# Writing the parts of q straight into the stacked operands of a rotary attention and gated MLP kernel

## The chip, the cores and the metric

The kernel runs on one core of a Trainium2 chip. The metric is the device time of one execution in microseconds (us), in which the inputs already lie in the chip's memory.

## What is computed

The reference, cut to what matters:

```python
# q, k, v: [8, 8, 576, 64] (batch, heads, positions, head size), float32
q_rot, k_rot = rotate(q), rotate(k)          # rotary embedding, halves of 32
scores = (q_rot @ k_rot.T) / sqrt(64)
attn = exp(scores - max(scores)); attn /= sum(attn) + 1e-9
x = concat_heads(attn @ v)                   # [8, 576, 512]
h = relu(x @ w_in)                           # [8, 576, 1024]
u, vv = h[..., :512], h[..., 512:]
vn = (vv - mean(vv)) / sqrt(var(vv) + 1e-6)  # over the 512 features
vs = w_spatial @ vn + b_spatial              # mixes the 576 positions
out = (u * vs) @ w_out                       # [8, 576, 512]
```

## The kernel before

The work is cut into 32 pairs of heads, four a batch, and eight MLPs, one a batch. TensorE (PE) makes every product; VectorE (DVE) takes row maxima, transposes the exponentials in blocks of 32 and scales; ScalarE (ACT) makes the exponentials, evacuates PSUM and rounds; GpSimd (POOL) multiplies by the rotary tables and subtracts; SyncE (SP) issues the transfers, from one queue, in order.

**High and low parts.** From pair 4 on, and in the whole MLP, a float32 operand is used as two shorter numbers: a high part, which ACT makes by copying into a rounded type (`round_hi`, line 424), and a low part, which is the operand minus its high part (`rest_lo`, line 427, on POOL). A product is high*high + low*high + high*low.

**Stacks.** A head has 64 rows, PE takes 128. So the two parts of one head's q stand above each other in one operand, and so do two copies of k's high part. For each head a of a pair:

- `qs[a]`: 64 rows of q's high part (the head's own rows) and 64 rows of its low part (the other rows), 512 positions;
- `ks[a]`: k's high part twice; `lks[a]`: k's low part on the own rows, zeros on the others.

`qs[a]` and `ks[a]` are two ranges of one wide tile, `stk0` for head 0 and `stk1` for head 1; both `lks` lie in `stk2`. They exist once, so pair i can fill them only when the scores of pair i - 1 have been made. The last 64 positions of each head don't fit into the four tiles of 128 and go together into one more tile: `qt` (high) and `ql` (low), multiplied with `lk` itself. That tile's scores come first in a pair, then four tiles for head 0 and four for head 1 (line 796).

**Preparing a pair** (`prepare`, from line 525). q and k of a pair are loaded into `st[0]` and `st[1]` (pool `stage`, three buffers for all pairs), each with its half-swapped copy in the columns from 576 on. POOL multiplies both by the tables (two operations of 576 columns, line 549) and adds them (line 553). ACT then rounds, POOL subtracts. For q the high part went to the upper columns of `st[0]` and the low part over the lower ones; for k both go to `lk`. From there ten transfers a pair fill the stacks: four of 128 KB for q, six of 144 KB for k. Four small ACT operations copy the end pieces of q into `qt` and `ql`.

**Order.** Each engine works through its instructions in program order. The order is written out: the table `ORDER` lists all operations by number, a letter behind a number names the engine where there is a choice, and `HOME` lists which buffer of its pool each new tile takes. An operation that has to wait holds up everything behind it on its engine, or on SyncE's queue.

Of the kernel before, what the change touches and what calls it, by code (L numbers as in the profile page):

```python
# [8 lines left out]
F32 = mybir.dt.float32  # L9
# [6 lines left out]
P = 128  # L16
# [79 lines left out]
def pool_ns(n):  # L96
# [4 lines left out]
6 5 2 3 0 9 8 1 12 4 7 11 135 13 137 136 61 63 67 10 68 69 70 139 141 71 72 73 140 74 75 138g 76 33 77 211 78 81 82 79 80 83 84 142g 85 86 87 88 89 90  # L101
15 305 16 17 144 147 212 145 215 42 97 14 98a 18 19 95 56 96a 93 94a 127 128 91 92a 100 101a 62 296 109 110a 99 143 494 306 20 21 104 307 129 102 213
103v 216 146 148 214 105a 106 107a 149 34 57 123 35 152 124a 118 108 150 153 151 36 37 120 38 39 121a 119a 59 309 311 154 24 25 115 116a 157 113 114a
111 26 117 155 158 27 28 29 30 156 112 130 122 125 58 159 126 162 22 167 160 217 218 168a 23 171 172v 163 161 164 165 166 169 173 174v 220 223 408 60
221 170a 287 40 203 204 205 219 176 177a 182 180 131 224 178 179v 222 175 308 185 225 181a 183a 184 43 228 226 186a 199 31 44 45 310 200v 229 418 132
187 51 133 46 47 48 424 227 425 426 430 134 189 390 190a 399 191 192a 230 231 188 49 194 41 195v 196 197a 232 193 198 233 64 206 207 431 417 234 235
238 201 202 503 243 239 236 237 240 245 246a 432 244v 241 247 312 248v 252 50 242 279 253v 256 249 280 254 208 255a 250a 209 288 289 281 314 441 315
316 317 318 210 251 257v 445 261 258 259a 262a 319 52 290 291 292 260 419 427 320 433 321 440 428 293 294 270 429 271a 322 323 267 268v 263 265 297
748 272 298 266a 324 434 436 755 269 264 754 756 273v 299 325 326 327 282 275 435 749 438 274 337 437 328 54 442 276v 341 329 300 301 302 342a 760 303
338v 283 277 278 330 331 757 334 439 332 313 339 340a 333 335 336 373 443 343 344v 444 446 447 448 53 352 353v 350 351a 374 761 375 450 409 410 295  # L110
284 348 451 758 345 452 304 759 349v 411 762 381 355 412 458 413 356a 459 449 346 347a 454 285 286 364 365a 455 354 764 765 453 824 460 359 357 360a
366 461 456 457 358 361 462 463 376 362a 377 830 825 466 467 363 369 367a 368 414 464 465 370a 371 468 469 372 831 470 471 420 421 422 382 423 378 763
# [139 lines left out]
    "11410020117631100051000131604005002120450000010076103100411001350101624000000000511700641100115600571400015200100720004100601750100101001137"  # L252
    "41051100010010170001041062011101001750110401310002150200074000720000401165007011200117132600101400071030000610501104704001100651000150700042"
    "60000116075401012032010051306100110500470000110010110612325400071001001031040026501000146070003001500401130060107011214630000700115440001160"
    "50011400702046360176541322756102153276142501607435164257406517423765406174501"
)


# [865 lines left out]
```

## Time and profile before

| what | value |
|---|---|
| median of three runs | 825.38 us (823.13 to 827.4) |
| the profiled execution: its own time | 820.87 us |
| its span, from first to last instruction | 818.6 us |
| PE / DVE / ACT / POOL busy | 98% / 69% / 65% / 69% of the span |
| granted TensorE clock | 0.997 of full speed |
| data moved by the transfer queue | 142.04 MB |

PE's busy time is that of its matmuls; loading the weights of the next matmul (PEld) overlaps it. Where a row names a releaser, it is what ended the wait, judged from the semaphores; "issue" means that the profile shows nothing that the engine waited for. Times in the rows are from the start of the span.

### The profile page before, as it was taken

Reading aid. Unit: us, or ns where it says so; the run is one execution under the profiler, and the core shown is the slowest. Engines: PE = TensorE matmul, PEld = TensorE weight load, DVE = VectorE, ACT = ScalarE, POOL = GpSimd, SP = SyncE. Lnnn points to the kernel's source line nnn. Section 1 sums busy time; section 2 is a strip of 40 time slices with the busy share of each in tenths; the row PEclk is TensorE's granted clock in tenths of the full one; section 3 lists DMA queues with packets and bytes.
Section 4 is the critical chain, followed back from the end, with each engine's and each line's share of the span. In section 5 each row is a group of like instructions: output and inputs, shape, how many; then the busy total and the mean of one; then the engine's idle time right before and its main releaser. Section 6 shows DMA issues by size and latency. Waiting matters only on the chain.

```text
span 818.6 us, 30242 instructions
## 1 busy us (share of the span) xinstructions
PE 799.3 (98%) x12568; PEld 722.2 (88%) x12568; DVE 561.6 (69%) x1134; ACT 535.6 (65%) x1380; POOL 567.7 (69%) x480
## 2 busy tenths in 40 slices
PE   7999999999999999999999999999999999999998
PEld 3666799998999989999999989999789988999898
DVE  5878997776866676667866579776676657764320
ACT  4998787666866578555865568666576657754442
POOL 6999897965958768665888566878468755823231
PEclk9999999999999999999999999999999999999999
DMA  9665766678767786779768679777856678562101
GB/s 356 231 214 164 182 184 175 164 192 218 193 179 189 195 215 161 175 174 235 189 173 210 160 202 216 174 194 189 226 139 168 176 186 220 126 140 79 44 2 58
DMA packets 62667, 144.56 MB, mean 177 GB/s; under 512 B 10945, under 2 KB 11201, under 8 KB 62530
## 3 DMA queue, kind: packets, MB, share of 16 engines
q1 hardware_dynamic: 62386, 142.04, 65.5%
q8 instruction: 99, 1.62, 0.9%
q10 hardware_dynamic: 144, 0.59, 0.2%
q14 instruction: 38, 0.31, 0.1%
HBM read 93.55 MB, written 9.58 MB: 126 GB/s over the span
## 4 chain that ended last, share of the span: by engine, by line
PE 84%; DMA 6%; SPq 3%; DVE 2%; POOL 2%; ACT 2%; issue 1%; ACTq 0%; POOLq 0%; DVEq 0%
PE psum L796 16%; PE psum L756 14%; PE psum L955 13%; PE psum L970 12%; PE psum L937 11%; PE psum L914 10%; PE psum L816 3%; PE psum L725 3%; SPq L421 3%; PE psum L679 2%; DMA st<-in_qk_dram 1%; DMA rb<-rt20d 1%; DMA stk<-lk 1%; DMA tabs<-in_tab_dram 1%; POOL st L549 1%
## 5 line engine op out<-in xcount | busy, mean ns | idle before, releaser
L838 DVE TENSOR_REDUCE nmx<-psum 128x1 f32<-128x576 f32 x288 | 212.8, 747 | 94.0 <-PE psum L796 78.8
L841 ACT ACTIVATE et<-psum,nmx 128x576 f32<-128x576 f32 x288 | 212.7, 740 | 90.0 <-DVE nmx L838 87.9
L843 DVE STREAM_TRANSPOSE et<-et 128x576 f32<-128x576 f32 x252 | 187.2, 761 | 40.5 <-ACT et L841 40.1
L549 POOL TENSOR_TENSOR st<-st,tabs 128x576 f32<-128x576 f32 x112 | 158.5, 1429 | 52.0 <-DMA st<-in_qk_dram 44.7
L756 PE MATMUL psum<-et,vr 32*64 32x144 f32 x8064 | 141.6, 285 | 0.9 <-issue 0.9
L756 PEld LDWEIGHTS psum<-et,vr 32*64 32x64 f32 x8064 | 126.3, 130 | 12.3 <-issue 10.3
L955 PE MATMUL psum<-wsp,vn 128*128 128x288 f32 x768 | 125.5, 296 | 0.0
L937 PE MATMUL psum<-x,wi 128*128 128x288 f32 x768 | 121.1, 296 | 0.3 <-ACT vn L424 0.2
L970 PE MATMUL psum<-g,wo 128*128 128x288 f32 x768 | 119.2, 296 | 1.1 <-issue 1.1
L914 PE MATMUL psum<-wi,x 128*128 128x512 f32 x448 | 118.0, 396 | 1.8 <-ACT vv L988 1.1
L937 PEld LDWEIGHTS psum<-x,wi 128*128 128x128 f32 x768 | 108.9, 188 | 4.7 <-issue 1.6
L970 PEld LDWEIGHTS psum<-g,wo 128*128 128x128 f32 x768 | 107.8, 188 | 3.8 <-issue 3.0
L955 PEld LDWEIGHTS psum<-wsp,vn 128*128 128x128 f32 x768 | 109.5, 188 | 1.5 <-issue 1.2
L796 PE MATMUL psum<-stk 128*128 128x288 f32 x448 | 99.2, 303 | 4.2 <-ACT et L841 1.5
L796 PE MATMUL psum<-stk,stk 128*128 128x288 f32 x448 | 96.3, 296 | 0.7 <-issue 0.6
L914 PEld LDWEIGHTS psum<-wi,x 128*128 128x128 f32 x448 | 79.5, 188 | 16.8 <-ACT x L772 1.6
L796 PEld LDWEIGHTS psum<-stk 128*128 128x128 f32 x448 | 72.5, 188 | 13.9 <-issue 4.9
L427 POOL TENSOR_TENSOR g<-u,g 128x288 fp32r<-128x288 f32 x64 | 51.1, 806 | 47.7 <-ACT g L424 47.7
L553 POOL TENSOR_TENSOR st<-st 128x576 f32<-128x576 f32 x56 | 79.7, 1427 | 2.9
L880 POOL TENSOR_TENSOR x<-x,rb 128x576 f32<-128x576 f32 x32 | 45.7, 1429 | 40.5 <-DVE nmx L838 10.2
L796 PEld LDWEIGHTS psum<-stk,stk 128*128 128x128 f32 x448 | 71.5, 188 | 0.3 <-DMA stk<-lk 0.3
L427 POOL TENSOR_TENSOR x<-x,x 128x576 fp32r<-128x576 f32 x64 | 54.5, 874 | 18.1 <-ACT x L424 17.9
(129 smaller groups left out, 1020.2 us busy)
## 6 DMA issues: line engine op xcount, KB each, us to landing
vr<-in_v_dram SPq DMA_DIRECT2D x116, 320.0 KB
st<-in_qk_dram SPq DMA_DIRECT2D x64, 576.0 KB
stk<-lk SPq DMA_DIRECT2D x168, 144.0 KB
stk<-st SPq DMA_DIRECT2D x112, 128.0 KB
out_dram<-ob SPq DMA_DIRECT2D x31, 288.0 KB
ws<-in_w_spT_dram SPq DMA_DIRECT2D x2, 576.0 KB
tabs<-in_tab_dram ACTq DMA_DIRECT2D x1, 576.0 KB
wi12raw<-in_w_in_dram SPq DMA_DIRECT2D x1, 512.0 KB
```

What stands on the lines that cost most here:

```text
L427: eng.tensor_tensor(out=lo, in0=src, in1=hi.bitcast(F32), op=ALU.subtract)
L549: f = lambda e: e.tensor_tensor(out=st[j][:, cols], in0=st[j][:, cols], in1=tabs[:, cols], op=ALU.mult)
L553: f = lambda e: e.tensor_tensor(out=st[j][:, :S], in0=st[j][:, :S], in1=st[j][:, S:2 * S], op=ALU.add)
L756: nc.tensor.matmul(bank(g)[64 * h:64 * h + 64, EACH // 9 * (1 - h):EACH // 9 * (1 - h) + EACH], lhsT=vr[rows, b % 4, b // 4, h, :], rhs=e[ ...
L796: nc.tensor.matmul(pt[:, c * 512:c * 512 + HALF], lhsT=lhsT, rhs=rhs[:, c * HALF:(c + 1) * HALF], start=(n == 0), stop=(n == len(parts) - 1))
L838: op(DVE, 680, key + K_MAX, lambda: nc.vector.tensor_reduce(out=nmx.tile, in_=tops(), op=ALU.max, axis=AX.XY, negate=True), r=[pt], w=[nmx ...
L841: op(ACT, 750, key + K_EXP, lambda: nc.scalar.activation(weights(), tops(turn), AF.Exp, bias=nmx.tile, scale=1.0, accum_out=sm[:, to:to + ...
L843: op(DVE, 705, key + K_TURN, lambda: nc.vector.transpose(out=blocks(et, at), in_=blocks(et, at)), w=[(et, at)])
L914: nc.tensor.matmul(pm.tile, lhsT=lhsT, rhs=win[1, d][:, j, :], start=(d == 0 and n == 0), stop=(d == 3 and n == len(todo) - 1))
L937: nc.tensor.matmul(pm[:, :HALF], lhsT=win[0, d][:, i, f * P:(f + 1) * P], rhs=x[d][:, at:at + HALF], start=(d == 0 and n == 0), stop=(d == ...
L955: nc.tensor.matmul(pm[:, :HALF], lhsT=lhsT, rhs=rhs, start=(t == 0 and n == 0), stop=(t == 4 and n == 1))
L970: nc.tensor.matmul(pm[:, :HALF], lhsT=wout[d,][:, i, m * P:(m + 1) * P], rhs=gs[d][:, at:at + HALF], start=(d == 0 and n == 0), stop=(d == ...
```

## The change

For pairs 4 to 31, `prepare` no longer makes q's parts inside `st[0]`. ACT rounds the 512 columns of each head straight into the own rows of `qs[a]`, and POOL writes the difference straight into the other rows, so that the four q transfers of a pair are gone; the six k transfers stay. The end pieces go from `st[0]` into `qt` by ACT and, as differences, into `ql` by POOL (formerly ACT copied both). `st[0]` is free when the last of these eight operations has read it. The operations are numbered and ordered anew (`ORDER`, `HOME`). In the first row of `wake`, `count` is a number for the maker of the order and not part of the program.

```diff
 ORDER = """
-6 5 2 3 0 9 8 1 12 4 7 11 135 13 137 136 61 63 67 10 68 69 70 139 141 71 72 73 140 74 75 138g 76 33 77 211 78 81 82 79 80 83 84 142g 85 86 87 88 89 90
...
+6 5 9 2 3 1 4 8 135 12 7 11 13 136 10 137 139 140 141 138g 142g 309 219 67 68 73 69 70 71 72 74 75 76 77 78 81 82 79 80 83 84 85 86 87 88 144 89 90 0
...
-        def hi(j, rows=slice(0, P)):
-
-            return st[0][rows, S:].bitcast(F32R) if j == 0 else lk[rows, S:]
-
-        def lo_q(e):
-            rest_lo(e, st[0][:, :S].bitcast(F32R), st[0][:, :S], hi(0))
-
-        def tails(part, to, one):
-            for h in range(2):
-                c0 = S * part + 4 * P * (1 - h)
-                one(sixteens(to, h), st[0][64 * h:64 * h + 64, c0:c0 + TW].bitcast(F32).rearrange("p (g i) -> p g i", g=4))
+        own, oth = (lambda a: slice(64 * a, 64 * a + 64)), (lambda a: slice(64 - 64 * a, P - 64 * a))
+        body = lambda a: st[0][own(a), a * TW:a * TW + 4 * P]
+        ends = lambda a: st[0][own(a), 4 * P * (1 - a):4 * P * (1 - a) + TW].rearrange("p (g i) -> p g i", g=4)
+
+        def high_ends():
+            for a in range(2):
+                round_hi(sixteens(qt, a), ends(a))
+
+        def low_ends(e):
+            for a in range(2):
+                rest_lo(e, sixteens(ql, a), ends(a), sixteens(qt, a))
...
-        op(ACT, 573, key - K_HIQ, lambda: round_hi(hi(0), st[0][:, :S]), r=[(st[0], 0)], w=[(st[0], 1)])
-        op(ACT, 535, key - K_TAIL, lambda: tails(1, qt, round_hi), r=[(st[0], 1)], w=["qt"])
-        pair_op(S, key - K_LOQ, lo_q, r=[(st[0], 1)], w=[(st[0], 0)])
-        op(ACT, 535, key - K_TAIL + 0.1, lambda: tails(0, ql, round_hi), r=[(st[0], 0)], w=["ql"])
...
-            for dst, rows, part, tok, dep in (
-                (qd, own, 1, ("qs", a, 0), (st[0], 1)), (kd, own, 1, ("ks", a, 0), (lk, 1)), (kd, oth, 1, ("ks", a, 1), (lk, 1)),
-                (ld, own, 0, ("lks", a), (lk, 0)), (qd, oth, 0, ("qs", a, 1), (st[0], 0)),
-            ):
...
+        op(ACT, 535, key - K_TAIL, high_ends, r=[(st[0], 0)], w=["qt"])
+        op(POOL, 2 * pool_ns(TW), key - K_TAIL + 0.1, lambda: low_ends(nc.gpsimd), r=[(st[0], 0), "qt"], w=["ql"], port=True)
         for a in range(2):
...
+            op(ACT, act_ns(4 * P), key - K_HIQ, lambda a=a: round_hi(qs[a][own(a), :], body(a)), r=[(st[0], 0)], w=[("qs", a, 0)])
+            op(POOL, pool_ns(4 * P), key - K_LOQ, lambda a=a: rest_lo(nc.gpsimd, qs[a][oth(a), :], body(a), qs[a][own(a), :]), r=[(st[0], 0), ("qs", a, 0)], w=[("qs", a, 1)], port=True)
...
+            for dst, rows, part, tok in ((kd, own(a), 1, ("ks", a, 0)), (kd, oth(a), 1, ("ks", a, 1)), (ld, own(a), 0, ("lks", a))):
...
-    op(PE, 3600, -90, wake, r=[("wsp", 0)], w=[idle], new=[idle], count=8)
+    op(PE, 3600, -90, wake, r=[("wsp", 0)], w=[idle], new=[idle], count=16)
```

What the new order does is seen best at two places. The first is SyncE's queue where it fills the stacks for pair 26; `st26_0` is that pair's q, `lk26` its k, and the number behind a name is a buffer's. Before:

```order
L421 DMA stk1_561<-st26_0_8846 64x512
L421 DMA stk2_562<-lk26_9389 64x576 x2
L421 DMA stk1_561<-lk26_9389 64x576
L421 DMA stk0_560<-st26_0_8846 64x512 x2
L421 DMA stk1_561<-lk26_9389 64x576
L421 DMA stk0_560<-lk26_9389 64x576
L421 DMA stk1_561<-st26_0_8846 64x512
L421 DMA st28_0_9721<-in_qk_dram 128x1152
L421 DMA st28_1_9724<-in_qk_dram 128x1152
```

The same place on the same queue in the changed kernel:

```order
L419 DMA vr25_9323<-in_v_dram 32x4x640
L419 DMA stk0_415<-lk26_9397 64x576 x2
L419 DMA stk1_416<-lk26_9397 64x576
L419 DMA stk2_417<-lk26_9397 64x576 x2
L419 DMA stk1_416<-lk26_9397 64x576
L419 DMA st27_0_9621<-in_qk_dram 128x1152
L419 DMA st28_0_9646<-in_qk_dram 128x1152
```

The four copies out of `st26_0` are gone, the two k copies for head 0 come first instead of fourth and last, and the loads behind them have changed places.

The second place is POOL around pairs 22 and 23, beside the MLP of batch 4 (`vn`, the normalised features, are its low parts). Before, with line 427 as the subtraction that makes q's low part inside `st23_0`:

```order
L549 TENSOR_TENSOR st23_0_7759<-st23_0_7759,tabs_64 128x576 x2
L427 TENSOR_TENSOR vn_71<-vv4_2_7824,vn_71 128x512
L553 TENSOR_TENSOR st23_0_7759<-st23_0_7759 128x576
L549 TENSOR_TENSOR st23_1_7893<-st23_1_7893,tabs_64 128x576
L427 TENSOR_TENSOR st23_0_7759<-st23_0_7759 128x576
L549 TENSOR_TENSOR st23_1_7893<-st23_1_7893,tabs_64 128x576
L553 TENSOR_TENSOR st23_1_7893<-st23_1_7893 128x576
L427 TENSOR_TENSOR vn_71<-vv4_3_7848,vn_71 128x512
L427 TENSOR_TENSOR lk23_8098<-st23_1_7893,lk23_8098 128x576
```

The same place on POOL in the changed kernel, with line 425 as the subtractions, line 547 as the products and 551 as the sums:

```order
L425 TENSOR_TENSOR stk1_416<-st22_0_7224,stk1_416 64x512
L547 TENSOR_TENSOR st23_1_7918<-st23_1_7918,tabs_64 128x576
L425 TENSOR_TENSOR stk0_415<-st22_0_7224,stk0_415 64x512
L547 TENSOR_TENSOR st23_1_7918<-st23_1_7918,tabs_64 128x576
L551 TENSOR_TENSOR st23_1_7918<-st23_1_7918 128x576
L425 TENSOR_TENSOR vn_71<-vv4_3_7817,vn_71 128x512
L425 TENSOR_TENSOR lk23_8063<-st23_1_7918,lk23_8063 128x576
```

The low part of pair 22's q now goes into the stacks at the time when the next pair's k is being turned, and for head 0 it stands behind the first product of that k, `st23_1`. Pair 30 is alike, with one more subtraction between:

```order
L547 TENSOR_TENSOR st31_1_11058<-st31_1_11058,tabs_64 128x576
L425 TENSOR_TENSOR vn_71<-vv6_2_11004,vn_71 128x512
L425 TENSOR_TENSOR stk0_415<-st30_0_10440,stk0_415 64x512
L425 TENSOR_TENSOR vt1_72<-vv6_4_11053,vt1_72 64x512
L425 TENSOR_TENSOR x28_11074<-x32_28_10873,x28_11074 128x576
```

There the stacks' row was moved behind the first product of `st31_1`, the k of pair 31.

## Rows read from the trace of the kernel before

**Rows 1.** The page: span, busy times, transfer queues, chain by engine.

```profile
span 818.6 us, 30242 instructions
...
PE 799.3 (98%) x12568; PEld 722.2 (88%) x12568; DVE 561.6 (69%) x1134; ACT 535.6 (65%) x1380; POOL 567.7 (69%) x480
...
q1 hardware_dynamic: 62386, 142.04, 65.5%
...
PE 84%; DMA 6%; SPq 3%; DVE 2%; POOL 2%; ACT 2%; issue 1%; ACTq 0%; POOLq 0%; DVEq 0%
```

**Rows 2.** Windows: start and end in us, length, each engine's busy us.

```profile
12.00:96.00 84.00, 81.22 (x605) 52.59 (x606) 72.34 (x119) 74.88 (x189) 77.56 (x65) 0.98 0.67 218
96.00:800.00 704.00, 696.31 (x11839) 651.90 (x11838) 482.88 (x1004) 452.64 (x1176) 482.71 (x398) 1.00 0.68 172
```

**Rows 3.** PE's waits from 20 us on: total us, times, longest us.

```profile
PE psum L796 <- ACT et L841: 2.0, 3, 1.2
PE psum L796 <- issue: 1.4, 2, 0.8
PE psum L796 <- DMA stk<-lk: 1.3, 1, 1.3
PE psum L914 <- ACT vv L988: 1.1, 1, 1.1
...
PE psum L725 <- DMA vr<-in_v_dram: 0.6, 1, 0.6
PE psum L796 <- DMA rt18d<-rt: 0.4, 1, 0.4
...
PE psum L816 <- issue: 0.2, 1, 0.2
```

**Rows 4.** The stacks' tile view: q transfers, min/median/max ns of an issue.

```profile
L421 SPq DMA_DIRECT2D stk<-st x112: 461/588/1465, 50.1 to 726.5; - x112
```

**Rows 5.** SyncE's timeline from 590 to 606 us: start us, us.

```profile
597.28 0.48 SPq L421 DMA_DIRECT2D stk<-st  x1
...
599.73 1.25 SPq L421 DMA_DIRECT2D stk<-st  x2
```

**Rows 6.** PE's timeline from 600 to 607 us; brackets: idle before, releaser.

```profile
605.48 0.50 PE L796 MATMUL psum<-stk 128*128 128x288 f32 x2 [1.27 <-DMA stk<-lk]
```

**Rows 7.** Groups by shape: busy us, mean ns of one; idle before, releaser.

```profile
L549 POOL TENSOR_TENSOR st<-st,tabs 128x576 f32<-128x576 f32 x112 | 158.5, 1429 | 52.0 <-DMA st<-in_qk_dram 44.7 <-DMA rb<-rt19d 6.9
L427 POOL TENSOR_TENSOR st<-st 128x576 fp32r<-128x576 f32 x28 | 39.9, 1426 | 11.6 <-ACT st L424 11.5
L424 ACT ACTIVATE st<-st 128x576 fp32r<-128x576 f32 x28 | 19.0, 677 | 5.8 <-POOL st L553 5.8
L424 ACT ACTIVATE ql<-st 64x64 fp32r<-64x64 f32 x56 | 14.0, 250 | 2.7 <-POOL st L427 2.3
L427 POOL TENSOR_TENSOR x<-x,x 128x64 fp32r<-128x64 f32 x32 | 10.4, 324 | 0.0
L427 POOL TENSOR_TENSOR vt<-vv,vt 64x512 fp32r<-64x512 f32 x8 | 10.3, 1287 | 11.7 <-ACT vt L424 11.4
L424 ACT ACTIVATE vt<-vv 64x512 fp32r<-64x512 f32 x16 | 9.5, 625 | 0.2
```

**Rows 8.** One window, columns as in rows 2 (POOL is the last engine).

```profile
60.00:180.00 120.00, 117.29 (x1777) 101.65 (x1779) 103.46 (x198) 91.41 (x232) 106.52 (x86) 1.00 0.69 179
```

**Rows 9.** VectorE's transposes: min/median/max ns, first and last start.

```profile
L843 DVE STREAM_TRANSPOSE et<-et x252: 720/768/781, 82.1 to 745.3; 128x576 f32<-128x576 f32 x126
```

**Rows 10.** Waits of all engines: total us, times, longest us.

```profile
POOL st L549 <- DMA st<-in_qk_dram: 44.7, 16, 7.5
...
ACT qt L424 <- PE psum L796: 7.4, 3, 4.2
```

**Rows 11.** Timelines of SyncE and POOL at one load of k.

```profile
473.01 0.35 SPq L421 DMA_DIRECT2D st<-in_qk_dram  x1
477.60 2.83 POOL L549 TENSOR_TENSOR st<-st,tabs 128x576 f32<-128x576 f32 x2 [2.93 <-DMA st<-in_qk_dram]
```

More of the change, by code (lines that the diff above doesn't have):

```diff
@@ L105 @@
[L105 to L108, printed above, removed]
@@ new lines @@
+15 16 17 93 97 94a 147 98a 211 212 95 96a 381 14 18 215 145 56 91 92a 148 19 100 101v 146 109 110a 33 99 59 127 305 102 103a 62 20 213 104 21 390 128
+105v 129 51 24 106 107a 34 216 57 35 149 42 123 152 306 143 124a 153 108 150 151 120 121a 36 37 60 38 217 218 39 25 118 119a 22 154 157 115 116a 113
+114a 26 158 111 155 117 122 27 28 29 311 130 58 156 296 125 30 112 126 159 162 310 160 167 171 172v 168a 164 165 169 170v 214 287 163 161 173 220 221
+223 307 417 166 203 174a 222 224 204 131 132 176 177a 178 179v 133 61 175 63 185 205 418 23 180 182 183a 181v 206 207 43 44 225 228 226 186a 424 134
@@ new lines @@
+229 227 184 399 425 426 40 45 199 200v 187 46 492 47 191 192a 48 65 31 189 190a 230 231 233 188 194 32 196 193 195a 312 197a 232 198 235 238 236 430
+201 234 434 240 241 202 435 239 237 243 245 249 246a 244v 308 250v 247 254 242 208 279 252 255v 280 248a 288 431 209 253a 289 281 41 256 408 314 317
+318 315 316 432 419 210 251 257v 282 428 427 261 429 258 319 259a 260 49 50 290 291 433 746 292 52 262a 265 320 321 293 294 267 53 322 323 436 439 442
+268v 270 271v 263 264 324 438 297 298 272 273a 266v 325 326 269 299 275 276a 274 327 437 747 300 301 328 341 342a 277 313 329 334 278 295 302 303 330
@@ L243 @@
+331 337 332 338v 333 339 340a 335 444 445 336 343 440 350 448 373 344v 352 753 351a 374 375 446 353a 409 410 348 449 752 756 450 447 345 355 304 820
+356a 456 754 755 758 349v 441 346 452 347a 411 359 457 458 364 365a 412 453 454 443 413 283 284 354 361 414 757 464 285 460 360v 286 362a 764 465 366
+376 377 367a 461 466 357 358 826 363 759 382 451 369 370a 766 767 459 420 421 422 368 765 371 768 462 372 455 463 468 469 378 470 379 472 473 474 467
[128 rows of a table added]
 """
 HOME = (
-    "07001001200210320112100321201701101262005314263544564504017201570341170151074205451200106107120672100013167465345740101501260002341620100436"
@@ new lines @@
+    "65230010600541201200105030147100011416010511300001702006001470001100006117300051140011306017140102607000002600700312154010710510615004002010"
+    "61610000524000000311450001000017610200401711061230001007110050040601001241100300221400720006010001175040010010260172010110104610710113600171"
+    "00001104540111560017020507100461100104020176010010001156010112001011140600000700000016130501101140011702003101150700402700010600051001131741"
+    "00160153207031000157440000001102006545110700110001401601062070002130500107163001141007120131400071000020601070002101000154311200076201010170"
@@ new lines @@
+    "14006000371006200001154207600105010001013215700041104000110506115400110700010104062010761000123610540001100011170600401021110701016011050110"
+    "00410701013065110010000016200004501020045000107012610010410012200730154100007001016050110014147500060100014020070002600006171540011202010170"
+    "36000401110710100001106000151002701311060410200010001631500423005000040107011610501016101007140006012100000007104501102570161040001402007662"
+    "00010001500161041720011105030600110000540017011600010000132511207430011011060015400001623005400011070061100031140011572300004100007116045014"
@@ L256 @@
+    "10051700101057406074651202756420317125007621513647065724261574603574601547160"
 )
@@ L564, in prepare @@
                 rope(j, slice(*part), eng)
-        op(ACT, 573, key - K_HIQ, lambda: round_hi(hi(0), st[0][:, :S]), r=[(st[0], 0)], w=[(st[0], 1)])
-        op(ACT, 535, key - K_TAIL, lambda: tails(1, qt, round_hi), r=[(st[0], 1)], w=["qt"])
-        pair_op(S, key - K_LOQ, lo_q, r=[(st[0], 1)], w=[(st[0], 0)])
-        op(ACT, 535, key - K_TAIL + 0.1, lambda: tails(0, ql, round_hi), r=[(st[0], 0)], w=["ql"])
-        op(ACT, 573, key - K_HIQ, lambda: round_hi(hi(1), st[1][:, :S]), r=[(st[1], 0), (st[1], 1)], w=[(lk, 1)], new=[lk])
@@ L571, in prepare @@
-        pair_op(S, key - K_LOK, lambda e: rest_lo(e, lk[:, :S], st[1][:, :S], hi(1)), r=[(st[1], 0), (lk, 1)], w=[(lk, 0)])
-        for a in range(2):
-            own = slice(64 * a, 64 * a + 64)
-            oth = slice(64 - 64 * a, P - 64 * a)
-            qd, kd, ld = lambda a=a: qs[a], lambda a=a: ks[a], lambda a=a: lks[a]
-            for dst, rows, part, tok, dep in (
-                (qd, own, 1, ("qs", a, 0), (st[0], 1)), (kd, own, 1, ("ks", a, 0), (lk, 1)), (kd, oth, 1, ("ks", a, 1), (lk, 1)),
-                (ld, own, 0, ("lks", a), (lk, 0)), (qd, oth, 0, ("qs", a, 1), (st[0], 0)),
-            ):
-                def copy(dst=dst, rows=rows, own=own, part=part, src=dep[0], c0=a * TW if dst is qd else 0, n=4 * P if dst is qd else S):
-                    load(dst()[rows, :].bitcast(F32), src[own, S * part + c0:S * part + c0 + n].bitcast(F32))
-                op(DMA, dma_ns(132, 1, 570, 2.9), key - (K_STACK2 if a else K_STACK), copy, r=[dep], w=[tok])
+        op(ACT, 535, key - K_TAIL, high_ends, r=[(st[0], 0)], w=["qt"])
@@ new lines, in prepare @@
+        op(POOL, 2 * pool_ns(TW), key - K_TAIL + 0.1, lambda: low_ends(nc.gpsimd), r=[(st[0], 0), "qt"], w=["ql"], port=True)
+        for a in range(2):
+            op(ACT, act_ns(4 * P), key - K_HIQ, lambda a=a: round_hi(qs[a][own(a), :], body(a)), r=[(st[0], 0)], w=[("qs", a, 0)])
+            op(POOL, pool_ns(4 * P), key - K_LOQ, lambda a=a: rest_lo(nc.gpsimd, qs[a][oth(a), :], body(a), qs[a][own(a), :]), r=[(st[0], 0), ("qs", a, 0)], w=[("qs", a, 1)], port=True)
+        high = lambda: lk[:, S:]
@@ new lines, in prepare, with copy @@
+        op(ACT, 573, key - K_HIQ, lambda: round_hi(high(), st[1][:, :S]), r=[(st[1], 0), (st[1], 1)], w=[(lk, 1)], new=[lk])
+        pair_op(S, key - K_LOK, lambda e: rest_lo(e, lk[:, :S], st[1][:, :S], high()), r=[(st[1], 0), (lk, 1)], w=[(lk, 0)])
+        for a in range(2):
+            kd, ld = lambda a=a: ks[a], lambda a=a: lks[a]
+            for dst, rows, part, tok in ((kd, own(a), 1, ("ks", a, 0)), (kd, oth(a), 1, ("ks", a, 1)), (ld, own(a), 0, ("lks", a))):
+                def copy(dst=dst, rows=rows, part=part, a=a):
+                    load(dst()[rows, :].bitcast(F32), lk[own(a), S * part:S * part + S].bitcast(F32))
+                op(DMA, dma_ns(132, 1, 570, 2.9), key - (K_STACK2 if a else K_STACK), copy, r=[(lk, part)], w=[tok])
```

19 lines of the change are left out of this document (2 added, 17 removed), and 258 rows, old and new, of the table ORDER.

## The prediction

> **What bounds the kernel now.** I read the page first: the span is 818.6 us, TensorE (PE) is busy in 98% of it, and each of the other engines in 65 to 69% [rows 1]. The chain that ended last is PE work for 84%. Then I cut the span into stretches [rows 2]. From 12 to 96 us PE, ScalarE (ACT) and GpSimd (POOL) are all nearly full: 81.2, 74.9 and 77.6 of 84 us. From 96 to 800 us PE is busy 696.3 of 704 us and everything else has room: POOL 482.7, ACT 452.6, VectorE (DVE) 482.9. So in the long middle PE sets the pace. The change adds and removes no matmul, and all that it could give back is PE's idle time: 84.0 - 81.2 = 2.8 us before 96 us and 704 - 696.3 = 7.7 us after, 10.5 us together. A change beside PE can cost more than that, since nothing bounds how long PE may be made to wait.
>
> Then I asked for whom PE waits [rows 3]: 2.0 us for exponentials on ACT, 1.1 us for ACT's evacuations of the MLP, 1.3 + 0.4 + 0.6 = 2.3 us for transfers, and in five lines, of which the first and the last stand there, 4.3 us that the profile puts down to nothing ("issue"). After the start PE never waits for POOL. Both sides of the change can be read from that: transfers cost PE 2.3 us now, POOL nothing.
>
> **What the change removes.** 112 transfers of 128 KB on SyncE's queue, four for each of the pairs 4 to 31. An issue holds that queue 588 ns in the median [rows 4]: 112 x 0.588 = 65.9 us less in the queue. The data is 112 x 128 KB = 14.7 MB of the queue's 142 MB, about a tenth of what keeps the DMA engines busy in 65.5% of the span [rows 1]. That is worth something only where PE ends up waiting for the queue. The clearest such place is at 605.5 us: PE sat idle 1.27 us for a transfer of k into the stacks [rows 6]. In front of it the queue issued a run of copies without a pause from 597.28 us on, among them q copies at 597.28 and two at 599.73 us [rows 5]. Those three are 0.48 + 1.25 = 1.73 us, more than the 1.27 us that PE waited. The order of the changed kernel has only the six k transfers there, so I take these 1.3 us as gained. The 0.4 us for a row of reciprocals and the 0.6 us for a tile of v go through the same queue, and I count them too: -2.3 us. The bounds are 0 (the next k transfer may wait for its own data) and all three.
>
> ACT loses 28 roundings of 128x576 (19.0 us) and 56 end pieces into ql (14.0 us); POOL loses 28 subtractions of 128x576 (39.9 us) [rows 7].
>
> **What it adds.** ACT rounds twice 64x512 per pair. The nearest row is the 64x512 rounding into vt, 625 ns: 56 x 0.625 = 35.0 us. ACT's sum is 35.0 - 19.0 - 14.0 = +2.0 us, 0.07 us per pair: nothing, with 704 - 452.6 = 251 us idle in the middle [rows 2].
>
> POOL subtracts twice 64x512 per pair. Its row of 64x512 takes 1287 ns, that of 128x576 over twice the partitions 1426 [rows 7]: the columns are paid for and not the partitions, so that splitting one operation by head nearly doubles it. 56 x 1.287 = 72.1 us. The ends are 56 pieces of 64x64; the nearest row is 128x64 with 324 ns, so 18.1 us. POOL's sum is 72.1 + 18.1 - 39.9 = +50.3 us, 1.8 us per pair: the largest term of the change, and it is on an engine that PE does not wait for now. What covers it is POOL's idle time, 704 - 482.7 = 221 us in the middle. The cover is thin in one stretch: from 60 to 180 us POOL is busy 106.5 of 120 us [rows 8], which leaves 13.5 us. The turned pairs' transposes run from 82.1 to 745.3 us [rows 9], so a pair takes some 663 / 28 = 23.7 us, and 120 us bring 5.1 pairs or 9.1 us. It fits if two thirds of the idle time can be used; if half can (6.7 us), POOL ends 2.4 us late there. I take 0 for this stretch, bounds 0 and 2.4.
>
> **What it moves.** The stacks for q exist once. Before, what waited for the previous pair's last scores was a copy on SyncE's queue; now ACT and POOL wait themselves, and whatever stands behind them on these engines waits too. By the order 31 of the 56 new ACT writes carry a wait for PE. Behind them stand exponentials and evacuations, but these feed a PE that is by then at the scores waited for. ACT already stops so three times, 7.4 us in all, at qt [rows 10], and PE loses at most the 2.0 us of [rows 3]. I take 0; the bound is that 7.4 us becomes PE's, were nothing else queued on PE.
>
> Worse is what stands ahead of a new subtraction. In pair 22 the subtraction for head 0 now stands behind the first product of the next pair's k, which needs a fresh load; in pair 30 likewise, with one product and a 128x512 subtraction between. POOL waited for such loads 16 times, 44.7 us in all [rows 10], 2.8 us each; one load was issued at 473.01 us and POOL went on with it at 477.60 us, 4.6 us later [rows 11]. A product takes 1.43 us [rows 7]. If PE stood at the scores when POOL began to wait, each place would cost 2.8 + 1.4 = 4.2 us; if POOL comes early enough, nothing. PE's own order is nearly what it was, and it has other products between the scores. I take 0.5 us each, nearer to nothing, since PE waits for POOL nowhere now; and 0.4 us for places where a subtraction of 1.29 us goes ahead of one that the MLP waits for. Together +1.4 us.
>
> The order anew moves most other instructions by a few places. I have no sign for that and take 0.
>
> **Sum.** -2.3 + 1.4 = -0.9 us. The profiled execution took 820.87 us (818.6 of span and 2.3 around it): 820.0 us. It lies 4.5 us under the median of the three runs, 825.38, so against the median I say **824.5 us**.
>
> **Rivals.**
> *It gets faster.* With the queue freer, the new order may also lose the 2.0 us for exponentials and half of the unexplained 4.3 us, 2.1 us, beside the 2.3 us, with no new wait: -6.4 us, 819.0. For it: these waits are short and local, and an order made anew with 66 us less in the queue can step round them. Against it: the same order must place 50 us more on POOL. Chance 0.32.
> *It gets slower, because POOL comes late.* Place: the subtractions of pairs 22 and 30 behind a load, and 60 to 180 us. Price: half of 4.2 us at both (4.2), 2.4 us in the full stretch, and no relief: +6.6 us, 832.0. It decides once POOL's lead on PE's scores at these places is under about 2 us. For it: POOL is the engine that gets the work. Against it: no wait of PE for POOL now, and 221 us of room. Chance 0.20.
> *VectorE is held up by the busier GpSimd.* The 252 transposes of VectorE take 720 to 781 ns, median 768 [rows 9], while POOL is busy for two thirds of the time: none was held up for as much as a tenth of its length. Were each that meets one of the added 50 us stopped for half an operation, 252 x 50.3/704 x 0.64 = 11.5 us of VectorE, at worst all on PE: 837. Chance 0.02. The Trainium skill (SBUF — State Buffer, Who interferes with whom) says that VectorE and GpSimd share a pair of ports under an exclusive lock, where the loser blocks for the whole instruction, and that a VectorE instruction with at most one SBUF input outside the two-port modes takes no part in it. By the lock alone the time would be those 837 us; by the exception it is unchanged. The trace agrees with the exception.
>
> **Chances and range.** No change, within 0.5% (4.1 us; about what a measurement of this kernel can tell from none): 0.46, at 824.5, itself from 821.3 to 829. Faster by more 0.32, slower by more 0.22 with VectorE's case. I leave out a tenth at each end: the low end passes the faster case by 2 us (817), since PE's whole 10.5 us would be 814.9; the high end is 830.5.
>
> **What would show it.** Right: no q copies on SyncE's queue; two 64x512 subtractions a pair on POOL near 1.29 us, POOL at about 618 us in all; PE idle for 5 to 9 us between 96 and 800 us; PE waits for transfers nearly gone. Wrong: a PE wait that ends at POOL's writes of the stacks, above all in pairs 22 and 30; the 64x64 pieces well above 324 ns; ACT's waits for PE at the stacks followed by PE waits for exponentials; transposes over 0.8 us. The forecast fails most easily through what I set to 0: the order made anew.

## The result and the profile after

The changed kernel takes 818.08 us (median of 6 runs, 815.88 to 819.1), the kernel before beside it 824.5 us (6 runs, 822.91 to 828.3). The ratio is 0.991, 95% interval 0.988 to 0.994: faster by 0.9%. Ratios here and below are made from the single executions in a kernel's faster state, not from the two medians, and differ a little from the medians' quotient. The forecast was 824.5 us, no change; the range (817 to 830.5) holds the result, but it came out in the faster case, to which I gave 0.32.

The page of the changed kernel (span, busy times, transfer queue, chain by engine), to be read against [rows 1]:

```profile
span 815.7 us, 30215 instructions
...
PE 800.5 (98%) x12568; PEld 722.7 (89%) x12568; DVE 562.0 (69%) x1135; ACT 538.0 (66%) x1351; POOL 618.8 (76%) x564
...
q1 hardware_dynamic: 53426, 127.35, 56.8%
...
PE 83%; POOL 8%; DVE 3%; DMA 2%; ACT 2%; issue 1%; SPq 0%; POOLq 0%; ACTq 0%; DVEq 0%
```

POOL does 51 us more and the queue moves 14.7 MB less. In the chain the 9% that belonged to DMA and SPq are down to 2%, and POOL's 2% have become 8%: the road to the last instruction no longer leads through the queue, but partly through GpSimd.

The same stretches as in [rows 2] and [rows 8], in the windows of the changed kernel (length, then busy us of PE, PEld, DVE, ACT, POOL):

```profile
12.00:96.00 84.00, 79.84 (x602) 52.07 (x603) 72.32 (x119) 72.48 (x182) 79.04 (x71) 0.99 0.63 199
96.00:800.00 704.00, 700.32 (x11865) 655.40 (x11864) 484.12 (x1007) 458.76 (x1159) 534.07 (x480) 1.00 0.58 153
...
60.00:180.00 120.00, 114.92 (x1698) 99.34 (x1695) 101.18 (x194) 91.88 (x225) 110.64 (x98) 1.00 0.59 157
```

In the long middle PE is idle for 704 - 700.3 = 3.7 us instead of 7.7 us. In the full part at the start it loses: 4.2 us idle from 12 to 96 us instead of 2.8, and 5.1 us instead of 2.7 from 60 to 180 us. The waits say for whom, to be read against [rows 3] (PE waits of the changed kernel after the first 20 us: total us, times, longest):

```profile
PE psum L791 <- ACT et L836: 2.2, 4, 1.2
PE psum L791 <- DMA stk<-lk: 1.6, 1, 1.6
PE psum L751 <- issue: 1.4, 3, 0.7
...
PE psum L791 <- POOL stk L425: 1.2, 1, 1.2
...
PE psum L932 <- DVE vv L986: 0.2, 1, 0.2
```

Gone are both waits at the scores marked "issue" (1.4 us), the one for k at 605 us (1.3), the rows of reciprocals (0.4), the tile of v (0.6) and those of the MLP for vv (1.1) and "issue". Two of over 1 us are new: for k's transfer of pair 4 at 77 us (1.6), so that the waits for transfers are not all gone, and for a GpSimd write of a stack in pair 7 (1.2). The exponentials stay at 2 us.

The profiled executions are only 3 us apart (span 818.6 and 815.7), the medians 6.4. Part of the gain is therefore in what the kernel before does in its other executions.

### The profile page after: what moved, and what is told of

It is laid out like the page before. It is cut to its first block, busy times and chain, and to the rows that moved or that the text cites. A ratio compares the mean times of both kernels' runs of the same rounds, so it can differ in the third digit from the quotient of the medians.

```text
span 815.7 us, 30215 instructions
## 1 busy us (share of the span) xinstructions
PE 800.5 (98%) x12568; PEld 722.7 (89%) x12568; DVE 562.0 (69%) x1135; ACT 538.0 (66%) x1351; POOL 618.8 (76%) x564
## 4 chain that ended last, share of the span: by engine, by line
PE 83%; POOL 8%; DVE 3%; DMA 2%; ACT 2%; issue 1%; SPq 0%; POOLq 0%; ACTq 0%; DVEq 0%
PE psum L791 16%; PE psum L751 14%; PE psum L950 14%; PE psum L909 12%; PE psum L965 12%; PE psum L932 9%; PE psum L720 2%; PE psum L811 2%; PE psum L674 2%; POOL st L547 2%; POOL stk L425 1%; ACT et L836 1%; DVE nmx L833 1%; DMA stk<-lk 1%; POOL x L875 1%
## 5 line engine op out<-in xcount | busy, mean ns | idle before, releaser
L425 POOL TENSOR_TENSOR stk<-st,stk 64x512 fp32r<-64x512 f32 x56 | 72.0, 1287 | 20.4 <-ACT stk L422 14.7
```

What stands on the lines that cost most here:

```text
L425: eng.tensor_tensor(out=lo, in0=src, in1=hi.bitcast(F32), op=ALU.subtract)
```

## Experiments

Three theories stood against each other. **Queue**: the time comes from the 112 transfers that are gone, as slots on SyncE's queue, as waits for their landing or as bytes. **Order**: it comes from the order made anew, whatever fills the stacks. **Both**: it needs the two together. Beside these stands the price of GpSimd's added 50 us. The experiments ran in three sets, each with runs of the kernel before on the same chip; its median there was 825.1 to 826.1 us (824.5 beside the changed kernel), so kernels are compared by the ratio, and 1% is about 8.25 us.

| kernel | median, us | ratio to before | 95% interval |
|---|---|---|---|
| changed kernel | 818.08 | 0.9911 | 0.9881 to 0.9940 |
| before, no q transfers | 817.21 | 0.9889 | 0.9864 to 0.9913 |
| before, q transfers of one row | 822.28 | 0.9956 | 0.9936 to 0.9976 |
| changed, four idle transfers of 128 KB a pair | 828.66 | 1.0037 | 1.0014 to 1.0060 |
| changed, four idle transfers of 2 KB a pair | 819.73 | 0.9921 | 0.9893 to 0.9949 |
| changed, GpSimd's q subtractions cut short | 817.37 | 0.9892 | 0.9868 to 0.9917 |
| changed, GpSimd's q subtractions made twice | 861.27 | 1.0431 | 1.0405 to 1.0457 |
| changed, four places of GpSimd swapped | 817.52 | 0.9902 | 0.9864 to 0.9939 |
| q transfers in the new order, two placements | 905.89, 875.53 | 1.0964, 1.0567 | 1.0926 to 1.1003, 1.0513 to 1.0621 |
| direct writes in the old order, two placements | 904.0, 880.98 | 1.0944, 1.0663 | 1.0907 to 1.0980, 1.0624 to 1.0703 |

### Order and writes apart: four transplants

Two kernels do the old work in the new order, two the new work in the old order. Their code is that of the one kernel, `ORDER` and `HOME` are those of the other, with the operations that only one of them has put in by hand:

```diff
 # the code of before
-ORDER, HOME = those of before
+ORDER, HOME = those of the changed kernel; each q transfer stands where the direct write stood
```

> The q transfers of before, four a pair, but every other operation in the order (and the buffers) of the changed kernel; the making of q's parts stands where the changed kernel has its direct writes. Queue theory (the gain comes from the 112 transfers that are gone): no gain, 823 to 826 us, ratio to before 0.998 to 1.002, and TensorE waits for transfers of 2 us or more. Order theory (the gain comes from the order made anew, whatever fills the stacks): 817 to 819 us, ratio 0.991 to 0.993. Theory that both are needed: no better than before, 824 us or more, since the freed places of the queue, round which the new order was made, are filled again.

> The direct writes of the changed kernel in the order (and the buffers) of before: ScalarE's and GpSimd's new operations stand where the q copies that they replace stood. Queue theory: the gain is there without the new order, 817 to 820 us, ratio 0.991 to 0.995. Order theory: no gain, 823 to 826 us. Theory that both are needed: 826 us or more, with TensorE waits that end at GpSimd's 64x512 writes of the stacks, since GpSimd's 50 us were not provided for in that order.

Measured: 905.89 and 904.0 us. Neither the queue nor the order theory had allowed for 80 us. The PE waits of the first (q transfers in the new order):

```profile
PE psum L796 <- ACT et L841: 26.2, 16, 5.2
PE psum L756 <- DMA vr<-in_v_dram: 15.8, 10, 3.9
```

and of the second (direct writes in the old order):

```profile
PE psum L791 <- POOL stk L425: 28.8, 10, 7.3
PE psum L791 <- ACT et L836: 9.3, 8, 2.6
```

In the second, PE stands before GpSimd's writes. In the first, I take it that a q transfer that waits for PE at an early place of the in-order queue holds up the loads of v behind it; this is not shown, since SyncE's waits for the scores are 102.3 us in all there and 107.6 us in the kernel before. Both are the cost of my places as much as of the order. So both were tried once more at better places: the transfers right behind the k transfers of their head, the writes as early as the last scores of the pair before allow. One piece of GpSimd's order, from the first to the second kernel with direct writes:

```diff
 L390 MEMSET stk_561 64x576 x2
+L425 TENSOR_TENSOR stk_559<-st_0_485,stk_559 64x512
+L425 TENSOR_TENSOR stk_560<-st_0_485,stk_560 64x512
 L640 TENSOR_TENSOR st_0_309<-st_0_309 128x576
```

> Again the q transfers of before in the order and buffers of the changed kernel, but each now stands right behind the first k transfer of its head, not where the changed kernel writes q's parts; so it no longer blocks SyncE's queue early. Queue theory: about as before, 822 to 828 us, ratio to before 0.998 to 1.004, with TensorE waits for transfers; the 80 us that the first such kernel lost came from its places on the queue. Order theory: 817 to 819 us. If it stays above 850 us, the order of the changed kernel does not suit the transfers at all, and this way of parting order and writes tells nothing.

> Again the direct writes in the order and buffers of before, but each write stands as early as the rotation of q and the last scores of the pair before allow, not where the q copy stood. Queue theory: the gain is there without the new order, 816 to 821 us, ratio to before 0.990 to 0.996. Order theory: 823 to 828 us. Theory that both are needed: well above before, with TensorE waits that end at GpSimd's writes, as in the first such kernel, where they were 28.8 us.

Measured: 875.53 and 880.98 us, 5.7% and 6.6% over before. By the bound written down ahead, the first tells nothing of the order theory. The second is well above before, as the theory that both are needed says, but the next runs get the gain without a new order. What the four show together is that an order written for one set of operations, with the other's put in by hand, costs 6 to 10%. Whether a new order made for the old operations would gain by itself can't be read from them.

### The transfers taken out of the kernel before

This parts the theories without touching an order. In one kernel the q transfers of pairs 5 to 31 move one row in place of 64, in the other there are none.

```diff
-load(dst()[rows, :].bitcast(F32), src[own, ...])
+one = (lambda s: slice(s.start, s.start + 1)) if i > 4 and n < S else (lambda s: s)
+load(dst()[one(rows), :].bitcast(F32), src[one(own), ...])
```

```diff
-load(dst()[rows, :].bitcast(F32), src[own, ...])
+if i == 4 or n == S:
+    load(dst()[rows, :].bitcast(F32), src[own, ...])
```

> The kernel before, its order and buffers untouched, with its q transfers for pairs 5 to 31 cut to one row each (2 KB for 128 KB); the other rows of the stacks keep what pair 4 left there, so the scores are not those of the reference. Every issue slot, every wait and every other operation stays. Bytes theory (what the 112 transfers cost TensorE are their 14.7 MB on the DMA engines): 816 to 821 us, ratio 0.989 to 0.995, the whole gain of the change without its order. Order theory: 823 to 828 us. Slots theory (the time on SyncE's queue): 823 to 828 us too, and the next run tells those two apart.

> The kernel before, order and buffers untouched, with no q transfers at all for pairs 5 to 31 (the stacks keep pair 4's q). Bytes theory: within 1.5 us of the run with one row each. Slots theory: 816 to 821 us here, against 823 to 828 there. Order theory: 823 to 828 us in both.

Measured: 822.28 us with one row (ratio 0.9956), 817.21 us with none (0.9889). With the order of before, and with all of ACT's and POOL's old work, taking the transfers out gives 1.1%, as much as the whole change (the intervals overlap). So a new order is not needed for the gain. The bytes are 0.44% of it (3.6 us), the slots and the waits for landing the other 0.67% (5.5 us); neither the bytes nor the slots theory was right alone.

Some of the second part can be seen at two places. In the kernel before, SyncE's timeline has two q copies, and PE's timeline the wait behind them that the profile puts down to "issue" (it stands in the 1.4 us of [rows 3]):

```profile
360.45 1.26 SPq L421 DMA_DIRECT2D stk<-st  x2
```

```profile
364.74 0.50 PE L796 MATMUL psum<-stk 128*128 128x288 f32 x2 [0.78 <-issue]
```

The same two rows in the kernel with one row a transfer:

```profile
362.84 1.23 SPq L421 DMA_DIRECT2D stk<-st  x2
```

```profile
367.26 0.50 PE L797 MATMUL psum<-stk 128*128 128x288 f32 x2 [0.81 <-issue]
```

PE reads the stack that the copies fill. It starts 364.74 - 361.71 = 3.03 us after the end of their issue with 64 rows, and 367.26 - 364.07 = 3.19 us with one. Without the transfers PE runs through, as its timeline in the third kernel shows:

```profile
363.51 1.48 PE L971 MATMUL psum<-g,wo 128*128 128x288 f32 x9
364.83 0.43 PE L797 MATMUL psum<-stk 128*128 128x288 f32 x2
```

So this "issue" was a wait for a transfer. The wait for k at 605 us, in which the prediction saw 1.3 us to gain [rows 6], stays with one row a transfer and goes without the transfers too. First one row, then none:

```profile
609.62 0.50 PE L797 MATMUL psum<-stk 128*128 128x288 f32 x2 [1.65 <-DMA stk<-lk]
```

```profile
604.24 0.54 PE L797 MATMUL psum<-stk 128*128 128x288 f32 x2
```

That 2 KB takes as long as 128 KB at these places does not mean that the size never counts. The trace also records when each of the sixteen parts of a transfer lands, and the packets that the DMA engines move:

| copy that PE waits for | all parts on record but the last landed by, us | end of a 16 KB packet | last part landed | PE's load of the stack starts |
|---|---|---|---|---|
| q, 64 rows | 363.45 | 363.32 | 364.65 | 364.71 |
| q, one row | 365.10 | 366.08 | 367.18 | 367.24 |
| k, q copies with 64 rows | 604.23 | 603.95 | 605.34 | 605.45 |
| k, q copies with one row | 607.92 | 608.21 | 609.49 | 609.59 |

The last packets of each copy start within 0.15 us of the end of a 16 KB packet from another queue, which the profile calls "instruction". So in all four rows PE waited for one part of sixteen that had stood behind that packet. Over pairs 5 to 31 (the 107 and 106 of 108 q copies whose landings can be told apart), from the end of the issue to the last landing it took 3.09 us in the median and 1.72 us at least with 64 rows, and 2.25 and 1.06 us with one.

The other waits marked "issue" are of another kind. Two of the kernel before:

```profile
581.30 2.22 PE L756 MATMUL psum<-et,vr 32*64 32x144 f32 x124 [0.94 <-issue]
...
584.76 0.29 PE L796 MATMUL psum<-stk,stk 128*128 128x288 f32 x1 [0.63 <-issue]
```

The first stands inside a run of 144 like matmuls. There are 99 of those 16 KB packets, one for every 256 of PE's 25,326 recorded instructions. In the order of these records, all five "issue" waits from 96 to 800 us but the one at 364 us lie a multiple of 256 apart, and each ends 1.2 to 1.5 us after such a packet. The same holds for 31 of 32 such waits in nine traces. So by all signs PE waited there for its own next instructions, 3.3 us in the kernel before and 1.4 in the changed one; no run changed those packets alone.

All PE waits of the kernel with no q transfers from 96 to 800 us, transfers no longer among them:

```profile
PE psum L757 <- issue: 1.9, 2, 1.4
PE psum L915 <- ACT vv L989: 1.2, 1, 1.2
PE psum L797 <- ACT et L842: 0.6, 2, 0.4
PE psum L938 <- DVE vv L992: 0.2, 1, 0.2
```

One reservation: with no transfers PE doesn't wait for the making of q either, so the 1.1% is the most that removing them could give.

### The transfers put back into the changed kernel

Here the order stays the new one. Four transfers a pair go back onto SyncE's queue, at fixed places behind k copies; they carry a table to a spare place in memory, and nobody waits for them. The second kernel moves one row of 2 KB at the same places.

```diff
+if tok[0] == "lks" or tok == ("ks", a, 0):
+    load(spare[a, part], tabs[own(a), :4 * P])
```

```diff
-    load(spare[a, part], tabs[own(a), :4 * P])
+    load(spare[a, part, :1], tabs[64 * a:64 * a + 1, :4 * P])
```

> The changed kernel with four transfers of 128 KB a pair put back on SyncE's queue, behind the first and the last k copy of each head; they write a spare place in memory that nobody reads. Queue theory: the gain goes, 822 to 825 us, ratio to before 0.997 to 1.001, TensorE waits at the scores for the k copies. Order theory: 817 to 819 us, ratio 0.991 to 0.994; SyncE's issue time grows by about 66 us to no effect.

> The changed kernel with four transfers a pair put back at the same places as in the run with 128 KB each (828.66 us), but of 2 KB each. If what those cost were the issue slots on SyncE's queue (0.59 us each, 66 us in all): 826 to 829 us as well. If it were the bytes (14.7 MB, a tenth of what the DMA engines move): 817 to 820 us, as the changed kernel. Order theory: also as the changed kernel.

Measured: 828.66 us (1.0037) with the bytes, 819.73 us (0.9921) with the slots alone. The new order does not keep its gain when the queue is as full as before, as the queue theory said, but the loss is larger than the 822 to 825 us that it named. The slots alone cost 0.1%, which can't be told from nothing; there is no one here who waits for these transfers to land. The bytes cost 1.2%, more than the 0.44% that they gave in the kernel before. The window and three of PE's waits with the 128 KB transfers:

```profile
96.00:800.00 704.00, 696.20 (x11816) 648.75 (x11815) 482.32 (x1003) 455.92 (x1153) 531.50 (x478) 1.00 0.64 173
```

```profile
PE psum L794 <- DMA stk<-lk: 1.6, 1, 1.6
PE psum L794 <- ACT et L839: 1.5, 5, 0.5
...
PE psum L794 <- ACT x L770: 1.0, 1, 1.0
```

PE is idle for 7.8 us in the middle, as in the kernel before, and 3.7 us in the changed one. The waits are spread: for k, for exponentials, for x. This profiled execution took 823.3 us, the shortest of the twelve; where a typical one loses its 5 us more is not on record.

### GpSimd's price and its room

```diff
-rest_lo(nc.gpsimd, qs[a][oth(a), :], body(a), qs[a][own(a), :])
+rest_lo(nc.gpsimd, qs[a][oth(a), :n], body(a)[:, :n], qs[a][own(a), :n])   # n: 64, in pair 4 512
```

```diff
-rest_lo(nc.gpsimd, qs[a][oth(a), :], body(a), qs[a][own(a), :])
+[rest_lo(nc.gpsimd, qs[a][oth(a), :], body(a), qs[a][own(a), :]) for _ in range(2)]
```

> The changed kernel with the 64x512 subtractions on GpSimd cut to 64 columns for pairs 5 to 31 (the low part of q is left unfinished): 54 x (1.287 - 0.324) = 52 us less on GpSimd, nothing else changed. If GpSimd's added 50 us cost TensorE time in the changed kernel: 814 to 817 us, 1 to 4 us under it. If they lie wholly in GpSimd's idle time or the waits move to other work, as in the run with four places swapped: 817 to 819 us.

> The changed kernel with each 64x512 subtraction on GpSimd made twice: 56 x 1.287 = 72 us more, GpSimd at 691 us of 816. If GpSimd has room: 818 to 822 us. If the changed kernel stands at the edge: over 828 us, with TensorE waits that end at GpSimd's writes of the stacks, first in the full stretch between 60 and 180 us.

Measured: 817.37 us with 52 us less on GpSimd (0.9892 against the changed kernel's 0.9911, the intervals overlap), 861.27 us with 72 us more. The 50 us of the change cost PE next to nothing; another 72 us cost 43 us. With them GpSimd is busy in 80% of its span, and PE's waits name it three times:

```profile
PE psum L791 <- ACT et L836: 10.4, 10, 2.2
PE psum L791 <- POOL stk L425: 6.1, 4, 3.6
PE psum L965 <- POOL g L425: 5.4, 4, 1.7
PE psum L791 <- POOL ql L425: 4.3, 2, 2.8
```

It had 221 us of room by the sum of idle time [rows 2], 122 us more work is well under that, and yet PE waits. The run can't tell GpSimd's load from delay, though: each doubled subtraction also makes the stack that PE reads next 1.29 us later. What speaks for load is that the waits for the MLP (`g`) and for ScalarE, which nothing doubled, have grown too.

### The one wait for GpSimd

The wait of pair 7 in the changed kernel, on POOL's timeline and then on PE's:

```profile
148.93 1.28 POOL L425 TENSOR_TENSOR stk<-st,stk 64x512 fp32r<-64x512 f32 x1
150.28 1.42 POOL L547 TENSOR_TENSOR st<-st,tabs 128x576 f32<-128x576 f32 x1
151.78 1.26 POOL L425 TENSOR_TENSOR stk<-st,stk 64x512 fp32r<-64x512 f32 x1
```

```profile
153.09 0.52 PE L791 MATMUL psum<-stk 128*128 128x288 f32 x2 [1.18 <-POOL stk L425]
```

A product of 1.42 us stands between the two subtractions, and PE waits 1.18 us for the second. The swap takes it out of the way, there and in pairs 22 and 30, and lets k's subtraction of pair 4 go first at 69 us:

```diff
+L425 TENSOR_TENSOR stk_415<-st_0_1192,stk_415 64x512
 L425 TENSOR_TENSOR stk_416<-st_0_1192,stk_416 64x512
 L547 TENSOR_TENSOR st_1_1737<-st_1_1737,tabs 128x576
-L425 TENSOR_TENSOR stk_415<-st_0_1192,stk_415 64x512
```

> The changed kernel with GpSimd's order changed at four places: the q subtraction of head 0 goes ahead of a rotary product in pairs 7, 22 and 30, and the k subtraction of pair 4 ahead of the subtraction for the spatial weights. If the order places GpSimd's work badly there: TensorE's wait of 1.2 us for GpSimd at 153 us and most of the 1.6 us for k at 77 us go, 814.5 to 816.5 us in median, 1.5 to 3 us under the changed kernel. If other work is as late at these places: 817 to 819 us, the waits move on. Pairs 22 and 30 showed no wait, so nothing from them.

Measured: 817.52 us (0.9902), not to be told from the changed kernel. PE's timeline of the swapped kernel says why:

```profile
153.16 0.53 PE L791 MATMUL psum<-stk 128*128 128x288 f32 x2 [0.28 <-ACT et L836]
...
157.42 0.66 PE L950 MATMUL psum<-wsp,vn 128*128 128x288 f32 x3 [1.00 <-DVE sgwo L469]
```

The 1.18 us are gone, and 4 us on PE waits 1.00 us for an operation with which VectorE prepares a weight (`sgwo`). Other work was as late; my expectation of 1.5 to 3 us is missed.

### A second profile of the kernel before

The kernel is the same, without an edit.

> The kernel before once more, for a second profile: its profiled execution took 820.87 us where its other runs have a median of 824.5. If the scatter is in the program's waits, this profile shows 822 to 827 us with TensorE idle 2 to 5 us longer than 10.5 between 12 and 800 us, and the longer waits are named; if it lies outside the span, the idle time is within 1 us of 10.5.

Measured: 825.98 us, span 823.7, 5.1 us more than in the first profile. The windows of the start and the middle, and the three longest PE waits of the middle:

```profile
12.00:96.00 84.00, 80.77 (x604) 52.62 (x603) 71.70 (x118) 74.38 (x189) 77.14 (x64) 0.97 0.67 217
96.00:800.00 704.00, 693.95 (x11803) 648.05 (x11802) 482.82 (x1003) 451.60 (x1174) 481.35 (x396) 1.00 0.68 172
```

```profile
PE psum L796 <- ACT et L841: 2.1, 4, 0.9
PE psum L796 <- issue: 2.0, 2, 1.4
PE psum L796 <- DMA stk<-lk: 1.4, 1, 1.4
```

PE is idle for 704 - 693.95 = 10.05 us here, 7.7 us in [rows 2]. From 12 to 800 us its idle time is 13.3 us against 10.5, 2.8 us more and so within the 2 to 5 us named for waits. At the scores it waits 2.1 + 2.0 + 1.4 = 5.5 us where the first profile has 0.3 (from 96 us on) + 1.4 + 1.3 = 3.0; 1.8 of the 2.5 us more are for exponentials. How much the waits cost is seen when the same matmuls are set beside each other, each time the first profile and then the second:

```profile
92.19 0.53 PE L796 MATMUL psum<-lk,qt 128*128 128x288 f32 x2 [0.55 <-ACT et L841]
```

```profile
92.82 0.53 PE L796 MATMUL psum<-lk,qt 128*128 128x288 f32 x2 [0.56 <-ACT et L841]
```

```profile
778.68 6.63 PE L937 MATMUL psum<-x,wi 128*128 128x288 f32 x48 [0.24 <-ACT vn L424]
```

```profile
783.68 6.64 PE L937 MATMUL psum<-x,wi 128*128 128x288 f32 x48 [0.25 <-ACT vn L424]
```

The second execution is 0.63 us behind at 92 us and 5.00 us at 779 us. So 4.4 of the 5.1 us are lost in the middle, and by the records of all matmuls they are lost in steps, at places where PE waits. Idle time shows only part of it. Without a wait a matmul starts before the ones in front of it are over (in the kernel with no q transfers at 364.83 us, while the nine ahead run to 363.51 + 1.48 = 364.99), and a wait takes this overlap away too. In the same way this execution loses some 7 us against the profiled one of the kernel with no q transfers (818.47 us): about 3 us where PE waits for transfers, at 369, 443 and 610 us, some 2.7 us for ScalarE and some 1.2 us at the blocks of 256 instructions. These are single executions; that ScalarE's part comes from the transfers is not shown.

## Why the prediction was right and wrong

**PE sets the pace, and its idle time is all there is to gain: right in kind.** The middle went from 7.7 to 3.7 us of idle time, less than the 5 to 9 us that were predicted. But the 10.5 us were the idle time of one execution, a short one, and a wait costs PE more than the idle time that it shows.

**What the removal is worth, "-2.3 us": the step that failed, by its size.** The transfers are worth up to 1.1%, some 9 us. The 1.3 us for k at 605 us were read rightly: that wait goes with the transfers. Two things were missed. First, I counted the waits that the profile puts down to transfers by name and left the 4.3 us of "issue" out of the sum. Of these only the one at 364 us, 0.78 us, was the landing of q copies, as the run with one row and the run with none show; the others from 96 us on, the second one at the scores among them, fall on PE's blocks of 256 instructions. Second, and more, I made the sum against one profiled execution, 820.87 us, and then added the 4.5 us up to the median as if the change left them alone. But the second profile shows that most of such a distance is waits of PE in the middle, above all for ScalarE, and that the landing at 364 us alone then costs 1.40 us of idle time:

```profile
368.67 0.50 PE L796 MATMUL psum<-stk 128*128 128x288 f32 x2 [1.40 <-issue]
```

After the change the profiled execution (817.52 us) lies 0.6 us under its median. Why the longer waits for ScalarE are not in the changed kernel is open.

**What the new operations take: right.** By shape in the changed kernel (busy us, mean ns; idle before), to be read against [rows 7]:

```profile
L425 POOL TENSOR_TENSOR stk<-st,stk 64x512 fp32r<-64x512 f32 x56 | 72.0, 1287 | 20.4 <-ACT stk L422 14.7 <-issue 1.3 <-POOL vn L425 0.8
L422 ACT ACTIVATE stk<-st 64x512 fp32r<-64x512 f32 x56 | 35.0, 625 | 7.0 <-PE psum L791 6.2
L425 POOL TENSOR_TENSOR ql<-st,qt 64x64 fp32r<-64x64 f32 x56 | 17.8, 318 | 4.1 <-ACT qt L422 1.9
L838 DVE STREAM_TRANSPOSE et<-et 128x576 f32<-128x576 f32 x252 | 186.7, 760 | 30.9 <-ACT et L836 30.5
```

The three sums were predicted as 72.1, 35.0 and 18.1 us, and POOL as a whole at 618, measured 618.8. ACT waits for PE at the stacks for 6.2 us in all, seven times, where the order had 31 places that could.

**What POOL's work costs PE, "+1.4 us": about the right size at the wrong place.** No wait of PE for POOL shows in pairs 22 and 30. The one there is lies in pair 7, inside the stretch from 60 to 180 us that I took as 0 with a bound of 2.4; PE loses 2.4 us more there than before, 1.2 of them for POOL. Most of the rest is the wait for k of pair 4, 1.6 us, which the prediction did not have. Cutting POOL's work short changed the time by 0.2%, which can't be told from nothing, and taking POOL's wait away only uncovered the next.

**"The order made anew", taken as 0: neither confirmed nor refuted as a gain, but not without weight.** The gain is there without it (before, no q transfers) and gone with it when the queue is full again (128 KB transfers put back). What it seems to do is to let PE run although POOL has 50 us more: in the old order, at the places that I tried, the same writes cost 7 to 9%. Up to 1.1% from the transfers, less a small price of GpSimd that the runs can't tell from nothing, agrees with the measured 0.9%; that the two add up so was not tested.

**The rivals.** The faster one named 819.0 us, 0.9 us from the result. The closeness is partly luck. Of its three parts the three named transfer waits went, but one of 1.6 us came; of the 4.3 us of "issue" 1.4 are left, but most of what went were not waits for the queue; the exponentials stayed (2.0 us before, 2.2 after). The rest of the 6.4 us lies in what the kernel before loses in its typical executions. The slower one, POOL late in pairs 22 and 30 and in the full stretch, didn't occur (1.2 us in pair 7 apart), though the run with its subtractions made twice shows that 72 us more on POOL would have set it off. VectorE was not held up: the transposes took 760 ns in the mean, against 761 ns before, with POOL busy for 51 us more:

```profile
L843 DVE STREAM_TRANSPOSE et<-et 128x576 f32<-128x576 f32 x252 | 187.2, 761 | 40.5 <-ACT et L841 40.1
```

**Open.** The same bytes cost 0.44% in the one kernel and 1.2% in the other. The idle transfers stand at other places and go to memory instead of the stacks; which of the two makes the difference was not tried. Nor was an order made anew for the old operations, nor PE's instruction packets moved out of the copies' way.

## What to carry to other kernels

A wait marked "issue" is not a wait for nothing, but it has more than one cause: look at what the waiting instruction reads and whether a transfer into it was issued shortly before, and at whether such waits lie a whole number of instruction blocks apart. Only the first kind is shown to go with the transfers. Where the executions of a kernel lie several us apart, take a second profile before you build a sum, and set matmul beside matmul, since idle time shows less than a wait costs. An on-chip copy through the queue stands on the chain with its landing, even with few bytes, so that writing the operand directly paid here although it added 50 us to an engine with room; but idle time summed over the span seems to overstate that room, and at the places tried here an order written by hand did not carry over to other operations.

## What was not expected of the hardware

In the four rows above, a 16 KB packet of instructions held back one part of sixteen of a copy by 1.1 to 2.1 us beyond the others, and PE waited for that part. Such a packet kept its DMA engine for 0.9 to 1.8 us in the kernel before and in the changed one. PE also waited at the edges of its blocks of 256 instructions, for 0.2 to 1.35 us at a time in the traces kept.

The Trainium skill (DMA: Bandwidth & Descriptors, Anatomy of one DMA — SWDGE (gpsimd) path) puts a fixed cost of about 2 us on each transfer, whatever its size, most of it for the confirmation that the last byte has landed. It says so of transfers that GpSimd issues; the copies here, of SyncE's queue, took at least 1.72 us from the end of their issue with 128 KB and 1.06 us with 2 KB, and in the median a good deal more. The prediction had no term for the landing or for PE's instructions.
